# A list scheduler that may hold every engine for higher-priority work, with later weight loads and a new priority sequence, in a fused attention and MoE kernel

## The chip, the cores and the metric

The kernel runs on one core of one Trainium2 chip. Its time is the device time in microseconds (us) of one execution. Each version is executed several times, and the median is quoted with the lowest and the highest run.

A core has four computing engines, which run side by side and wait for one another by semaphores: TensorE (PE in the profile, and PEld for its weight loads), VectorE (DVE), ScalarE (ACT) and GpSimd (POOL). SyncE (SP) issues most of the DMA transfers here, and GpSimd issues the loads of the weights.

## The reference, cut to what matters

```python
# attention: batch 4, heads 8, seq 768, head_dim 64, float32
k_chunks = k.reshape(B, H, nc, 32, D)                 # 24 chunks of 32 keys
k_min, k_max = np.min(k_chunks, axis=3), np.max(k_chunks, axis=3)
ub = np.sum(np.maximum(q * k_min, q * k_max), axis=-1)     # (broadcast, cut)
ub = np.where(causal, ub, -1e9)
top_chunks = np.argsort(ub, axis=-1)[..., -6:]        # each query keeps 6 chunks
scores = scale * np.matmul(q, k.transpose(0, 1, 3, 2))
attn = softmax(np.where(selected_and_causal, scores, -1e9))
x = np.matmul(attn, v)                                # to 3072 x 512
# MoE layer: w_in 512 x 2048, w_out 2048 x 512
h = x @ w_in
g = h * np.clip(h + 3.0, 0.0, 6.0) / 6.0
return g @ w_out
```

## The kernel before

The kernel works on 16 pairs of heads and, after every four pairs, on two groups of 384 tokens of the MoE layer. It is written as about 1,100 small operations. Each has an engine, an estimated duration, the operations that it depends on and a name. A list scheduler, which runs when the kernel is built, picks the order on every engine. The names, for pair `i`:

- `k`, `q`, `v`: the loads of K, Q and V, two transfers of 192 KB each. `C` is GpSimd's cast of V.
- `K`, `Q`: transposes on TensorE (tiles KT and QT), copies to SBUF on ScalarE (KTS, QTS), and then on VectorE two reductions of K (KM, KC) and a maximum with zero of Q (QP). `B` and `R` are casts to bf16.
- `U`: the upper bounds (tile UBP). `V`: their transposes (UBQ), twelve searches for the eight largest (MAX8) and a comparison (SEL). `L`: the transposes of SEL (SLT) and a copy (SELT).
- `S`: the scores in six pieces (SPS), the exponential on ScalarE (PT) and a causal mask on GpSimd. `P`: probabilities times V (PVP), and the division (Xb).
- `X`: the transposes of the layer's input (XT), for batch 0 on TensorE and for the others by DMA. `H`: the product with w_in (HP, 8 matmuls a block), a ReLU on ScalarE and a product on VectorE (GT). `O`: the product with w_out (OP, 4 matmuls a block).
- `w0` to `w7`: the eight weight loads of 512 KB, four of w_in (WIN) and four of w_out (WOUT), issued by GpSimd.

The scheduler, with its rule for holding an engine:

```python
def run(self, slack):
    # (cut: lists of candidates for each engine)
    while any(cand.values()):
        best = None
        for eng, lst in cand.items():
            mine = None
            for op in lst:
                r = self.ready(op)
                if r is None:
                    continue
                at = max(r, self.free[eng])
                if eng == "PE" and op.mode != self.mode:
                    at += SWITCH                      # 0.095 us
                s = slack.get(eng, 0.0)
                if mine is None or (at + s < mine[0]) or (at < mine[0] + s and op.key < mine[1].key):
                    mine = (at, op)
            if mine is not None and (best is None or mine[0] < best[0]):
                best = mine
        # (cut: place the operation, take its buffers, free its successors)
...
order = plan.run(dict(PE=0.1))
```

`op.key` is the place of the operation's name in one long text, SEQUENCE. On an engine without slack, whatever can start first goes first. On an engine with slack, an operation of higher priority may make the engine wait up to that long.

The weights, the DMA transposes and the loads:

```python
WGATE = (0, 2, 1, 5, 6, 5, 6, 2)      # weight load n waits for the cast of V of this pair

def plan_weights():
    for n in range(4):
        iss = add("POOL", 0.63, f"w{n}", lambda c=c: nc.gpsimd.dma_start(WIN[...], wi[...]),
                  deps=[st[WGATE[n]]["o_v"]], chain="wi")
        res.append(add("LD", 3.1, "", None, deps=[iss], chain="w"))
    # (cut: WOUT the same, with WGATE[n + 4])

s["ldk"] = add("LD", 2.07, f"k{i}", lambda: ld(i, s["ks"], k, "KS"), take=[s["ks"]], chain="ldk")
s["ldq"] = add("LD", 2.07, f"q{i}", lambda: ld(i, s["qs"], q, "QS"), take=[s["qs"]], chain="ldq")

for t in range(TPG):                  # three DMA transposes of 128x512 bf16 for a group
    nc.sync.dma_start_transpose(xt.obj[:, t], xb[b].obj[:, blk0 + t, :])
    ops.append(add("LD", 0.7, f"X{g}.{t}", tr, deps=norms[b] + ops[:1], ...))
```

The softmax here doesn't subtract the row's maximum and nothing guards it: scores larger than these inputs give would overflow.

Of the kernel before, what the change touches and what calls it, by code (L numbers as in the profile page):

```python
# [10 lines left out]
ACT = mybir.ActivationFunctionType  # L11
# [31 lines left out]
class Plan:  # L43
# [39 lines left out]
    def run(self, slack):  # L83
        cand = {}
        after = {}
        for op in self.ops:
            op.left = len(op.deps)
            for d in op.deps:
                after.setdefault(d, []).append(op)
            if not op.left:  # L90
                cand.setdefault(op.eng, []).append(op)
        order = []
# [6 lines that stand above are left out]
                    if r is None:  # L99
                        continue  # L100
                    at = max(r, self.free[eng])
                    if eng == "PE" and op.mode != self.mode:
                        at += SWITCH
                    s = slack.get(eng, 0.0)
                    if mine is None or (at + s < mine[0]) or (at < mine[0] + s and op.key < mine[1].key):
# [3 lines that stand above are left out]
            if best is None:  # L109
                raise RuntimeError("no order")  # L110
            at, op = best
            cand[op.eng].remove(op)
            op.at, op.end = at, at + op.dur
            self.free[op.eng] = op.end
            if op.eng == "PE":
                self.mode = op.mode
            for b in op.take:
                b.slot = self.count[b.ring] % len(self.rings[b.ring])
                self.rings[b.ring][b.slot] = b
                self.count[b.ring] += 1  # L120
            for d in after.get(op, ()):
                d.left -= 1
                if not d.left:
                    cand.setdefault(d.eng, []).append(d)
            order.append(op)
        assert len(order) == len(self.ops)
        return order
# [4 lines left out]


SEQUENCE = """
H6.10 H7.14 Q10 H7.12 H7.4 P5.1 H3.6 P10.1 q15 P12.1 K9 S8.1 O6.1.8 v12 X7.2 O3.0.12 v0 H3.8 H6.14 q10 X3.2
S10.1 S11.1 K4 O3.0.4 R0 U4 L13 P10.0 U10 S9.0 P4.1 S6.4 S0.3 q14 L11 H6.0 Q15 O6.1.4 P9.1 Q5 O6.1.12 q0 v2
O3.2.0 S0.0 q2 P9.0 k10 H2.12 Q11 S5.1 V5 H7.0 S7.0 L0 X1.0 H2.14 V9 P8.0 K8 k14 H7.10 v9 H3.0 X2.1 H0.10 H3.4
v10 K0 q1 U3 S4.4 S13.1 R8 X3.1 R5 C7 H2.4 O1.2.12 C1 S0.5 S6.3 H2.10 O2.0.4 v13 K13 k1 K10 H6.12 B1 O6.0.12 R1
O4.1.0 O6.0.8 P6.0 H3.10 H1.14 X6.1 O7.0.8 O6.2.4 w5 H7.6 S12.0 V4 O6.0.0 O1.0.12 H0.14 O3.2.8 V10 B7 k9 Q14
O2.1.0 O4.2.8 H2.6 S9.3 R10 S8.5 P8.1 H0.6 S0.1 S2.1 L5 U0 H1.10 B3 S12.1 O1.0.8 K6 V2 U15 O3.1.4 C0 H1.12 K11  # L140
L4 P11.0 S0.4 S9.1 H0.0 k15 H4.0 O4.0.0 U2 Q2 P13.1 H0.2 w0 V12 H1.2 B4 U9 O0.0.12 H0.4 v3 O5.1.0 W0 S8.2 S10.2
Q8 X4.2 H0.12 H6.6 B9 O5.0.0 B15 k6 S2.2 L12 R3 P1.1 w6 X4.1 O1.1.12 O5.2.0 S7.2 k3 H6.4 W2 O4.0.12 q12 O4.1.12
q13 X3.0 S8.3 H3.12 L2 S11.4 v11 Q3 V1 S10.4 U5 O3.1.8 S14.5 O1.0.4 S6.2 L14 q7 C5 O7.1.12 k8 U8 k11 O4.1.8
O3.1.12 S14.0 O2.0.12 q8 S3.3 S6.0 Q12 Q1 S2.4 C13 P13.0 P7.0 S9.4 K1 H6.2 O1.2.4 v8 O1.1.8 V15 P15.1 O1.2.0 R12
H5.12 O5.1.12 H7.2 S5.0 v15 O2.0.8 O0.1.4 H2.2 X2.2 X1.2 X7.0 O7.1.8 k0 H2.0 R11 S11.0 S7.1 O7.2.12 B5 w7 H3.14
S1.3 S8.4 H7.8 X7.1 S14.3 S4.3 H4.8 S4.1 O4.0.4 S2.5 U6 B8 X5.2 S15.5 O2.2.0 k13 v6 S5.3 S7.5 q6 S8.0 S9.2 K15
v4 H1.8 H5.2 k2 q4 P0.1 U7 S5.4 v5 P7.1 O4.2.12 S6.5 v7 O3.1.0 O0.1.0 q5 P3.1 O1.2.8 O5.0.8 H0.8 S4.5 S7.4 S1.4
L7 V3 S3.1 O3.0.8 S1.1 V7 O0.1.12 S7.3 k7 B13 H5.10 S2.0 S3.0 P1.0 S11.5 U13 P11.1 O6.2.8 W1 V8 O4.2.4 P4.0 V13
S4.0 V11 O7.0.4 Q6 H2.8 B10 C15 k5 S13.0 X2.0 O0.0.0 U1 O2.2.8 U12 P6.1 O3.2.12 L8 L6 U14 O6.2.12 P14.0 S10.3 Q4
S5.5 S9.5 P2.0 K2 C8 w4 w3 O6.1.0 X6.2 V6 S14.1 O0.1.8 k4 S14.2 S10.0 R13 S6.1 U11 B12 P2.1 S5.2 O4.1.4 O3.0.0  # L150
S13.2 O2.1.8 P12.0 X5.1 C14 K12 O2.2.12 O2.1.12 L15 H1.6 H6.8 H3.2 L1 H5.0 K3 H4.4 V0 q11 H4.6 O2.1.4 v14 C6 L9
H4.10 O7.1.4 B6 S15.3 H4.2 C3 O6.2.0 S4.2 O7.2.0 H1.0 C10 O0.2.0 O7.1.0 X4.0 S0.2 C11 C2 B2 S11.3 O5.1.4 O4.0.8
w1 H5.14 S13.5 O6.0.4 P5.0 S10.5 S15.1 P14.1 O7.2.8 L3 K14 P0.0 H4.12 O5.1.8 R7 S12.4 S3.5 O2.0.0 S12.5 S12.3 R4
O0.0.4 K5 C9 S11.2 C12 O7.0.12 O4.2.0 S15.4 Q13 R9 R2 S12.2 O0.2.12 V14 O1.1.0 O3.2.4 S1.2 q3 X6.0 H4.14 R14 L10
B14 S3.2 R15 S3.4 B0 H1.4 X5.0 R6 q9 C4 Q0 S14.4 B11 w2 X0.0 v1 k12 H5.8 S1.5 H5.6 O1.1.4 O0.0.8 K7 P15.0 O0.2.4
O5.0.4 O5.2.4 S15.2 O5.2.8 S13.3 O1.0.0 S13.4 O0.2.8 S1.0 S15.0 O5.2.12 O2.2.4 O7.0.0 O5.0.12 Q9 H5.4 Q7 P3.0
S2.3 X0.2
"""
POS = {tok: n for n, tok in enumerate(SEQUENCE.split())}

# [6 lines left out]
def kernel(  # L167
# [21 lines left out]
    Q0 = TOPK * CH  # L189
# [11 lines left out]
    plan = Plan(rings, dict(PE=1.4, DVE=3.2, ACT=2.2, POOL=9.3, LD=0.3, ST=0.0), place)  # L201
    add = plan.add
# [88 lines left out]
                       take=[s["vs"]], chain="ldv")  # L291
        s["o_v"] = add("POOL", 0.86, f"C{i}", castv, deps=[s["ldv"]], take=[s["vb"]], use=[s["vs"]], chain="castv")

    WGATE = (0, 2, 1, 5, 6, 5, 6, 2)

    def plan_weights():
        wi = moe_w_in.rearrange("(k p) f -> p k f", p=P)
# [2 lines left out]
        for n in range(4):  # L300
            c = n * (DFF // 4)
            iss = add("POOL", 0.63, f"w{n}",
                      lambda c=c: nc.gpsimd.dma_start(WIN[:, :, c:c + DFF // 4], wi[:, :, c:c + DFF // 4]),
                      deps=[st[WGATE[n]]["o_v"]], chain="wi")
            iss.gate = n
# [13 lines left out]
        for j in range(NBLK):  # L319
            nc.tensor.transpose(T[:, j * P:(j + 1) * P], src.obj[:, j].rearrange("p e d -> p (e d)"), IDENT32[:])  # L320

    UDUR = 0.70

    def plan_K(i):
        s, tok = st[i], f"K{i}"
# [167 lines left out]
    norms = [[] for _ in range(B)]  # L493
# [39 lines left out]
    def plan_mlp(g, wdma):  # L533
        tok0 = g * GRP
        b = tok0 // S
        blk0 = (tok0 - b * S) // P
        xt, gt = Buf("xt"), Buf("gt")

        def do_xt():
            ops = []  # L540
            if b >= XDMA:
                for t in range(TPG):
                    def tr(t=t):
                        if t == 0:
                            new(xt, [P, TPG, KT_HID, P], BF16, "XT")
                        nc.sync.dma_start_transpose(xt.obj[:, t], xb[b].obj[:, blk0 + t, :])  # L546
                    ops.append(add("LD", 0.7, f"X{g}.{t}", tr, deps=norms[b] + ops[:1], take=[xt] if t == 0 else [],
                                   use=[xb[b]] if t == 0 else [xb[b], xt]))
                return ops
            for k0 in range(0, KT_HID, 2):  # L550
                ps = Buf("sm")

                def tr(k0=k0, ps=ps):
                    T = new(ps, [P, 2, GRP], BF16, "XTP")
                    for kk in range(2):
                        for t in range(TPG):
# [12 lines left out]
            return ops
# [113 lines left out]
            plan_P(i, e)  # L683
    for b in range(B):
        plan_mlp_batch(b, wdma)
    order = plan.run(dict(PE=0.1))
    done_const = False
    for n, op in enumerate(order):
        if not done_const and op.eng not in ("LD",):
# [34 lines left out]
```

## Time and profile before

| | before |
|---|---|
| time, median of 3 runs | 301.73 us (301.5 to 302.09) |
| span of the profiled execution | 300.2 us |
| TensorE busy | 96% |
| ScalarE, VectorE, GpSimd busy | 59%, 55%, 31% |

From the page of the kernel before: the busy time of each engine with its share of the span; TensorE's clock and the DMA share in 40 slices of 7.5 us each, in tenths; and the group of the HP matmuls (busy time, mean ns of one, then the idle time just before them and what ended it).

```profile
PE 287.3 (96%) x2948; PEld 178.4 (59%) x2970; DVE 163.6 (55%) x448; ACT 178.3 (59%) x219; POOL 92.5 (31%) x168
...
PEclk9959999999999999999999999999999999999999
DMA  9999999999507999762400005201011015001112
...
L578 PE MATMUL HP<-XT,WIN 128*128 128x384 bf16 x512 | 86.0, 326 | 1.4 <-DMA XT<-Xb 1.0
```

TensorE sets the time. The DMA rings are full for the first 75 us or so. One slice of the clock row shows a 5: there TensorE ran at half its clock. The view of stretches gives that stretch (its columns are the bounds, the length, busy time and instructions of PE, PEld, DVE, ACT and POOL, then the granted clock, the DMA share and GB/s).

```profile
16.40:23.20 6.80, 6.64 (x78) 3.49 (x66) 3.67 (x19) 4.15 (x5) 3.68 (x7) 0.50 1.15 183
```

The Trainium skill, "TensorE: Matmul & The Clock Gate", Part 1, says that the clock is halved after an idle window of about 3.4 us. The trace agrees as to the length: the stretch is two such windows long.

From the view of waits of the kernel before: what TensorE waited for, the us in total, how many times, and the longest one.

```profile
PE SLT L438 <- DVE SEL_130 L421: 0.9, 1, 0.9
PE QT L320 <- DMA QS<-in_q_dram: 0.8, 1, 0.8
PE KT L320 <- DMA KS<-in_k_dram: 0.3, 1, 0.3
...
PE HP L578 <- DMA XT<-Xb: 1.0, 1, 1.0
```

From the timeline of the kernel before, the prologue. Columns are the start, the busy time, the engine, the line, the operation, out<-in, the shape and the count; the bracket gives the idle time ahead of it and what ended that.

```profile
13.40 1.16 DVE L418 MAX8 T_288<-UBQ 96x8 f32<-96x24 f32 x12
...
15.05 0.44 DVE L421 TENSOR_TENSOR SEL_130<-UBQ,T_288 96x288 bf16<-96x288 f32 x1
...
15.55 0.30 PE L438 MATMUL SLT<-IDENTB,SEL_130 96*128 96x96 bf16 x3 [0.94 <-DVE SEL_130 L421]
...
17.14 0.29 DVE L442 COPY SELT<-SLT 128x288 bf16<-128x288 bf16 x1
...
18.13 1.02 ACT L479 ACTIVATE PT<-SPS 128x1024 bf16<-128x1024 f32 x1 [2.68 <-PE SPS L473]
```

This chain on VectorE decides when the first exponential may start, at 18.13 us. And from the timeline of the last third of the kernel before (SPq is SyncE's queue, which issues the DMA):

```profile
244.62 5.15 SPq L546 DMA_TRANSPOSE XT<-Xb  x4
...
249.87 0.53 SPq L613 DMA_DIRECT2D out_dram<-OT  x1
...
250.44 2.53 SPq L546 DMA_TRANSPOSE XT<-Xb  x2
...
251.15 1.46 PE L578 MATMUL HP<-XT,WIN 128*128 128x384 bf16 x8 [1.01 <-DMA XT<-Xb]
```

HP of group 6 needs three transposes. SyncE issues four before the store, because the first transpose of group 7 was put between them, and TensorE waits.

**A ledger of lost time.** Busy shares hide small holes, so the document also uses sums over TensorE's own starts. Its work is read as blocks (six transposes of K, one `U`, one `P`, eight matmuls of `H`, and so on). Each block has a nominal length: the 5th percentile of the distance from its start to the start of the next one (1298 ns for a block of `H`, 665 for `P`, 655 for the transposes of K or Q). Block by block, the start minus all nominal lengths before it is the time lost so far. The nominal sum is 263.1 us in both kernels, because they do the same matmuls. The kernel before lost the other 37.0 us, including 4 us until the first transpose.

### The profile page before, as it was taken

The numbers are of one execution on the slowest core, as the hardware profiler recorded it, in microseconds if no ns is written. First come the engines' busy times: TensorE is split into PE (matmuls) and PEld (weight loads), VectorE is DVE, ScalarE is ACT, GpSimd is POOL, SyncE is SP. The second block draws the span as 40 slices with busy tenths as digits, with TensorE's granted clock in tenths as the row PEclk, the third lists the DMA queues.
The fourth block names the chain that finished last, engine by engine and source line by source line (L and its number), as shares of the span: only waits on it lengthen the run. The fifth ranks groups of instructions, "written<-read, shape, count | busy, mean of one in ns | idle before, by whom it ended". The sixth has DMA issues, their size and how long they took to land.

```text
span 300.2 us, 7214 instructions
## 1 busy us (share of the span) xinstructions
PE 287.3 (96%) x2948; PEld 178.4 (59%) x2970; DVE 163.6 (55%) x448; ACT 178.3 (59%) x219; POOL 92.5 (31%) x168
## 2 busy tenths in 40 slices
PE   7899999999999999999999999999999998999994
PEld 7657577765666556566555664566555654655444
DVE  4768887756669876236857461468421551625300
ACT  1557798987556358755766772565567832654311
POOL 8756776662106135531220342021133100000000
PEclk9959999999999999999999999999999999999999
DMA  9999999999507999762400005201011015001112
GB/s 172 218 185 217 203 210 193 220 196 198 89 0 184 243 228 206 156 134 68 107 35 3 35 12 130 72 0 37 13 60 37 2 31 144 2 1 71 37 70 71
DMA packets 92914, 32.20 MB, mean 107 GB/s; under 512 B 85584, under 2 KB 89936, under 8 KB 92880
## 3 DMA queue, kind: packets, MB, share of 16 engines
q1 hardware_dynamic: 87088, 27.14, 42.1%
q0 software_dynamic: 4224, 4.19, 8.8%
q10 hardware_dynamic: 1568, 0.39, 0.7%
q8 instruction: 23, 0.38, 0.6%
q14 instruction: 11, 0.09, 0.1%
HBM read 27.26 MB, written 6.29 MB: 112 GB/s over the span
## 4 chain that ended last, share of the span: by engine, by line
PE 82%; DVE 4%; ACT 4%; DMA 3%; SPq 2%; issue 2%; POOL 1%; ACTq 0%; DVEq 0%; POOLq 0%
PE HP L578 28%; PE OP L604 22%; PE PVP L509 8%; PE SPS L468 7%; PE SPS L473 5%; PE UBP L388 4%; PE QT L320 3%; PE KT L320 3%; ACT PT L479 2%; PE UBQ L410 2%; SPq L546 2%; DMA XT<-Xb 2%; DMA KS<-in_k_dram 1%; PE OP L625 1%; PE SLT L438 1%
## 5 line engine op out<-in xcount | busy, mean ns | idle before, releaser
L479 ACT ACTIVATE PT<-SPS 128x1024 bf16<-128x1024 f32 (+1 forms) x96 | 82.3, 924 | 18.7 <-PE SPS L473 15.2
L588 DVE SCALAR_TENSOR_TENSOR GT<-U,HP 128x768 bf16<-128x768 bf16 x64 | 60.8, 953 | 54.4 <-ACT U L582 49.3
L578 PE MATMUL HP<-XT,WIN 128*128 128x384 bf16 x512 | 86.0, 326 | 1.4 <-DMA XT<-Xb 1.0
L604 PE MATMUL OP<-WOUT,GT 128*128 128x512 bf16 x346 | 82.6, 379 | 1.6 <-issue 0.3
L582 ACT ACTIVATE U<-HP,THREE 128x768 bf16<-128x768 f32 x64 | 57.7, 901 | 33.4 <-PE HP L578 33.2
L578 PEld LDWEIGHTS <-WIN 128*128 128x128 bf16 x512 | 49.4, 98 | 35.1 <-issue 2.2
L483 POOL TENSOR_SCALAR_AFFINE_SELECT PT<-PT 128x256 bf16<-128x256 bf16 x96 | 38.6, 408 | 73.5 <-ACT PT L479 72.9
L604 PEld LDWEIGHTS <-GT 128*128 128x128 bf16 x368 | 34.4, 98 | 39.1 <-issue 1.7
L610 ACT ACTIVATE OT<-OP 128x512 f32<-128x512 f32 x23 | 13.7, 597 | 45.4 <-PE OP L604 43.6
L468 PE MATMUL SPS<-RHS,LHS 64*128 64x512 bf16 (+3 forms) x256 | 34.5, 315 | 1.4 <-ACT PT L479 1.3
L473 PE MATMUL SPS<-SELT,EM 64*128 64x288 bf16 (+6 forms) x384 | 32.8, 253 | 0.2 <-DVE SELT L442 0.2
L509 PEld LDWEIGHTS <-PT 128*128 128x128 bf16 x672 | 23.3, 98 | 4.5 <-issue 1.5
L473 PEld LDWEIGHTS <-EM 64*128 64x128 bf16 x384 | 18.9, 96 | 8.1 <-issue 1.1
L375 POOL CAST RHS<-QTS 128x768 bf16<-128x768 f32 x16 | 15.1, 951 | 26.7 <-ACT QTS L365 26.1
L514 DVE RECIPROCAL RINV<-PVP 128x6 f32<-128x6 f32 x32 | 6.1, 192 | 30.5 <-PE PVP L509 30.3
L468 PEld LDWEIGHTS <-LHS 64*128 64x128 bf16 x256 | 11.7, 95 | 14.2 <-issue 10.7
L354 POOL CAST LHS<-KTS 128x768 bf16<-128x768 f32 x15 | 12.6, 847 | 23.0 <-ACT KTS L335 22.8
L519 DVE TENSOR_TENSOR Xb<-PVP,RINV 128x384 bf16<-128x384 f32 x32 | 17.7, 555 | 0.9
L365 ACT COPY QTS<-QT 128x768 f32<-128x768 f32 x16 | 12.4, 802 | 6.6 <-PE QT L320 5.1
L339 DVE TENSOR_REDUCE KM<-KTS 128x24 f32<-128x768 f32 x15 | 13.9, 943 | 4.4 <-ACT KTS L335 4.3
L335 ACT COPY KTS<-KT 128x768 f32<-128x768 f32 x15 | 11.9, 807 | 5.2 <-PE KT L320 5.2
L320 PE MATMUL KT<-IDENT_114,KS 128*128 128x128 f32 x96 | 13.5, 284 | 0.5 <-DMA KS<-in_k_dram 0.3
(113 smaller groups left out, 233.6 us busy)
## 6 DMA issues: line engine op xcount, KB each, us to landing
VS<-in_v_dram SPq DMA_DIRECT2D x32, 192.0 KB, 4.6
KS<-in_k_dram SPq DMA_DIRECT2D x31, 192.0 KB, 4.5
QS<-in_q_dram SPq DMA_DIRECT2D x31, 192.0 KB, 4.5
out_dram<-OT SPq DMA_DIRECT2D x23, 256.0 KB, 2.0
WIN<-in_moe_w_in_dram POOLq DMA_DIRECT2D x4, 512.0 KB, 7.2
WOUT<-in_moe_w_out_dram POOLq DMA_DIRECT2D x4, 512.0 KB, 10.9
XT<-Xb SPq DMA_TRANSPOSE x18, 2.5
out_dram<-OT SPq DMA_DIRECT2D x2, 128.0 KB, 1.7
```

The lines of the kernel that those rows point to most:

```text
L320: nc.tensor.transpose(T[:, j * P:(j + 1) * P], src.obj[:, j].rearrange("p e d -> p (e d)"), IDENT32[:])
L375: nc.gpsimd.tensor_copy(new(s["rhs"], [P, S], BF16, "RHS")[:], qts.obj[:])
L468: nc.tensor.matmul(T[:, e, c:c + hi - lo], lhsT=s["lhs"].obj[e * D:(e + 1) * D, j * P:(j + 1) * P], rhs=s["rhs"].obj[e * D:(e + 1) * D, lo ...
L473: nc.tensor.matmul(T[:, e, c:c + hi - lo], lhsT=EM[e * D:(e + 1) * D, h, j * P:(j + 1) * P], rhs=s["selt"].obj[e * D:(e + 1) * D, x:x + hi ...
L479: nc.scalar.activation(T[:, :, 0:w], sp.obj[:, :, 0:w], ACT.Exp, scale=scale)
L483: nc.gpsimd.affine_select(out=dv, in_=dv, pattern=[[0, 2], [1, P]], compare_op=A.is_ge, fill=0.0, base=0, channel_multiplier=-1)
L509: nc.tensor.matmul(T[:, qb, :], lhsT=t[:, e, c:c + P], rhs=fx(s["vb"])[:, e, j, :], start=(j == 0), stop=(j == qb))
L519: nc.vector.tensor_tensor(out=xb[b].obj[:, :, h * D:(h + 1) * D], in0=pv.obj[:, :, 0:D], in1=s[("ri", e)][:].to_broadcast([P, NBLK, D]), o ...
L578: nc.tensor.matmul(T[:, f, 0:GRP].rearrange("p (t s) -> p t s", s=P), lhsT=WIN[:, kt, (f0 + f) * P:(f0 + f + 1) * P], rhs=xt.obj[:, :, kt, ...
L582: nc.scalar.activation(new(u, [P, 2, GRP], BF16, "U")[:], hp.obj[:, :, 0:GRP], ACT.Relu, bias=THREE[:], scale=1.0)
L588: nc.vector.scalar_tensor_tensor(out=gt.obj[:, f0:f0 + 2, :], in0=u.obj[:], scalar=6.0, in1=hp.obj[:, :, 0:GRP], op0=A.min, op1=A.mult)
L604: nc.tensor.matmul(T[:, :], lhsT=gt.obj[:, f, t * P:(t + 1) * P], rhs=WOUT[:, f, :], start=(f == 0), stop=(f == FT - 1))
```

## The change

The intent is that any engine may wait shortly for a part of higher priority, not only TensorE; that the loads of K, Q and V have the DMA rings to themselves early, so the first weights come after the fourth cast of V; that loads which could start together follow their priority (a hold of 0.01 us); and that a new sequence, searched for under these rules, is used. Three durations of the plan were corrected as well: `U`, the DMA transposes (0.7 to 1.3 us), and the cost of a change of TensorE's mode.

```diff
 LAT = {"PE": 0.22, "DVE": 0.09, "ACT": 0.09, "POOL": 0.09, "LD": 2.0, "ST": 2.0}
 SWITCH = 0.095
+SLACK = dict(PE=0.1, ACT=0.15, DVE=0.15, POOL=0.15, LD=0.01)
...
-                    if eng == "PE" and op.mode != self.mode:
+                    if eng == "PE" and self.mode not in (op.mode, 2):
                         at += SWITCH
...
 SEQUENCE = """
-H6.10 H7.14 Q10 H7.12 H7.4 P5.1 H3.6 P10.1 q15 P12.1 K9 S8.1 O6.1.8 v12 X7.2 O3.0.12 v0 H3.8 H6.14 q10 X3.2
+S3.2 q2 q1 O4.1.4 k13 O7.0.4 H3.2 P4.1 H7.12 P10.1 P6.0 U14 P5.0 O3.0.0 H3.8 R5 S0.5 O7.0.12 w0 H7.10 O7.1.8
 (some 20 lines cut: every name has a new place)
-    WGATE = (0, 2, 1, 5, 6, 5, 6, 2)
+    WGATE = (3, 1, 3, 5, 3, 1, 3, 0)
-    UDUR = 0.70
+    UDUR = 0.60
-                    ops.append(add("LD", 0.7, f"X{g}.{t}", tr, ...
+                    ops.append(add("LD", 1.3, f"X{g}.{t}", tr, ...
-    order = plan.run(dict(PE=0.1))
+    order = plan.run(SLACK)
```

What the engines then do early, by the order of instructions:

```
            before                                      after
TensorE     ... V0 K2 Q2 L0 U1 S0.3 S0.0 S0.5 ...       ... V0 K2 L0 Q2 U1 S0.5 S0.1 S0.2 ...
VectorE     ... U0 K1 K1 V0 Q1 K1 V0 K2 K2 L0 ...       ... U0 K1 V0 V0 K1 K1 Q1 L0 K2 U1 ...
ScalarE     B0 Q0 K1 ...                                Q0 B0 K1 ...
GpSimd      ... R2 C0 w0 S0.3 ...                       ... C2 B5 S1.4 (6 masks) C3 w0 R4 w1 ...
SyncE       ... k2 q2 v0 k3 q3 v1 k4 q4 v2 ...          ... k2 q2 v0 k3 v1 k4 q3 k5 v2 ...
```

More of the change, by code (lines that the diff above doesn't have):

```diff
@@ L134 @@
 SEQUENCE = """
-H6.10 H7.14 Q10 H7.12 H7.4 P5.1 H3.6 P10.1 q15 P12.1 K9 S8.1 O6.1.8 v12 X7.2 O3.0.12 v0 H3.8 H6.14 q10 X3.2
-S10.1 S11.1 K4 O3.0.4 R0 U4 L13 P10.0 U10 S9.0 P4.1 S6.4 S0.3 q14 L11 H6.0 Q15 O6.1.4 P9.1 Q5 O6.1.12 q0 v2
-O3.2.0 S0.0 q2 P9.0 k10 H2.12 Q11 S5.1 V5 H7.0 S7.0 L0 X1.0 H2.14 V9 P8.0 K8 k14 H7.10 v9 H3.0 X2.1 H0.10 H3.4
-v10 K0 q1 U3 S4.4 S13.1 R8 X3.1 R5 C7 H2.4 O1.2.12 C1 S0.5 S6.3 H2.10 O2.0.4 v13 K13 k1 K10 H6.12 B1 O6.0.12 R1
-O4.1.0 O6.0.8 P6.0 H3.10 H1.14 X6.1 O7.0.8 O6.2.4 w5 H7.6 S12.0 V4 O6.0.0 O1.0.12 H0.14 O3.2.8 V10 B7 k9 Q14
@@ L140 @@
-O2.1.0 O4.2.8 H2.6 S9.3 R10 S8.5 P8.1 H0.6 S0.1 S2.1 L5 U0 H1.10 B3 S12.1 O1.0.8 K6 V2 U15 O3.1.4 C0 H1.12 K11
-L4 P11.0 S0.4 S9.1 H0.0 k15 H4.0 O4.0.0 U2 Q2 P13.1 H0.2 w0 V12 H1.2 B4 U9 O0.0.12 H0.4 v3 O5.1.0 W0 S8.2 S10.2
-Q8 X4.2 H0.12 H6.6 B9 O5.0.0 B15 k6 S2.2 L12 R3 P1.1 w6 X4.1 O1.1.12 O5.2.0 S7.2 k3 H6.4 W2 O4.0.12 q12 O4.1.12
-q13 X3.0 S8.3 H3.12 L2 S11.4 v11 Q3 V1 S10.4 U5 O3.1.8 S14.5 O1.0.4 S6.2 L14 q7 C5 O7.1.12 k8 U8 k11 O4.1.8
-O3.1.12 S14.0 O2.0.12 q8 S3.3 S6.0 Q12 Q1 S2.4 C13 P13.0 P7.0 S9.4 K1 H6.2 O1.2.4 v8 O1.1.8 V15 P15.1 O1.2.0 R12
@@ L145 @@
-H5.12 O5.1.12 H7.2 S5.0 v15 O2.0.8 O0.1.4 H2.2 X2.2 X1.2 X7.0 O7.1.8 k0 H2.0 R11 S11.0 S7.1 O7.2.12 B5 w7 H3.14
-S1.3 S8.4 H7.8 X7.1 S14.3 S4.3 H4.8 S4.1 O4.0.4 S2.5 U6 B8 X5.2 S15.5 O2.2.0 k13 v6 S5.3 S7.5 q6 S8.0 S9.2 K15
-v4 H1.8 H5.2 k2 q4 P0.1 U7 S5.4 v5 P7.1 O4.2.12 S6.5 v7 O3.1.0 O0.1.0 q5 P3.1 O1.2.8 O5.0.8 H0.8 S4.5 S7.4 S1.4
-L7 V3 S3.1 O3.0.8 S1.1 V7 O0.1.12 S7.3 k7 B13 H5.10 S2.0 S3.0 P1.0 S11.5 U13 P11.1 O6.2.8 W1 V8 O4.2.4 P4.0 V13
-S4.0 V11 O7.0.4 Q6 H2.8 B10 C15 k5 S13.0 X2.0 O0.0.0 U1 O2.2.8 U12 P6.1 O3.2.12 L8 L6 U14 O6.2.12 P14.0 S10.3 Q4
@@ L150 @@
-S5.5 S9.5 P2.0 K2 C8 w4 w3 O6.1.0 X6.2 V6 S14.1 O0.1.8 k4 S14.2 S10.0 R13 S6.1 U11 B12 P2.1 S5.2 O4.1.4 O3.0.0
-S13.2 O2.1.8 P12.0 X5.1 C14 K12 O2.2.12 O2.1.12 L15 H1.6 H6.8 H3.2 L1 H5.0 K3 H4.4 V0 q11 H4.6 O2.1.4 v14 C6 L9
-H4.10 O7.1.4 B6 S15.3 H4.2 C3 O6.2.0 S4.2 O7.2.0 H1.0 C10 O0.2.0 O7.1.0 X4.0 S0.2 C11 C2 B2 S11.3 O5.1.4 O4.0.8
-w1 H5.14 S13.5 O6.0.4 P5.0 S10.5 S15.1 P14.1 O7.2.8 L3 K14 P0.0 H4.12 O5.1.8 R7 S12.4 S3.5 O2.0.0 S12.5 S12.3 R4
-O0.0.4 K5 C9 S11.2 C12 O7.0.12 O4.2.0 S15.4 Q13 R9 R2 S12.2 O0.2.12 V14 O1.1.0 O3.2.4 S1.2 q3 X6.0 H4.14 R14 L10
@@ L155 @@
-B14 S3.2 R15 S3.4 B0 H1.4 X5.0 R6 q9 C4 Q0 S14.4 B11 w2 X0.0 v1 k12 H5.8 S1.5 H5.6 O1.1.4 O0.0.8 K7 P15.0 O0.2.4
-O5.0.4 O5.2.4 S15.2 O5.2.8 S13.3 O1.0.0 S13.4 O0.2.8 S1.0 S15.0 O5.2.12 O2.2.4 O7.0.0 O5.0.12 Q9 H5.4 Q7 P3.0
-S2.3 X0.2
+S3.2 q2 q1 O4.1.4 k13 O7.0.4 H3.2 P4.1 H7.12 P10.1 P6.0 U14 P5.0 O3.0.0 H3.8 R5 S0.5 O7.0.12 w0 H7.10 O7.1.8
+X7.2 H7.4 W2 k7 q6 O6.0.12 H0.10 w5 P4.0 H3.4 V9 U6 U1 O4.0.12 U5 S0.1 O7.2.0 P15.0 H7.14 k11 S14.2 S5.1 S6.1
+U10 v0 P0.1 Q7 H2.8 P1.0 k1 Q3 k3 B4 Q10 P7.0 B3 S7.0 O7.2.12 H1.12 O5.2.12 O3.2.8 K10 S1.3 R3 U7 H0.6 P11.1 C2
@@ new lines @@
+P8.1 H1.2 P13.0 S7.5 H1.8 U2 Q8 L8 S7.2 q11 R4 C15 H3.0 S4.0 L1 S4.1 H7.8 S10.0 V3 S7.1 k0 v6 S12.1 S9.5 X4.2
+S12.5 S14.1 S1.1 S13.4 v3 S8.4 C7 P3.0 S4.2 S4.3 S10.2 O6.0.8 L12 O6.2.8 q0 H7.2 k10 S7.4 S6.4 X3.0 U8 X4.0 B12
+V0 S11.2 Q6 O5.1.0 R15 H2.0 S14.5 S1.2 K1 O6.0.0 X3.2 v1 V5 O0.2.12 L6 S5.5 O3.2.12 P10.0 O0.2.4 U4 U13 K15 H6.4
+S11.3 v7 U0 Q1 K5 k4 S2.3 R2 S14.4 B10 H2.12 q12 S9.0 q3 O7.2.8 R9 O7.0.8 U11 H5.14 X7.0 S12.2 w1 P2.0 H6.6
+O2.0.8 O0.1.8 K12 L5 X1.2 B7 L11 B15 q14 R7 C4 H2.6 O1.2.8 P5.1 Q5 H1.4 H5.8 S3.3 S10.3 V2 H3.6 U3 O3.2.4 P9.0
@@ new lines @@
+V15 S8.1 Q2 P11.0 w3 S6.0 X0.0 U9 P3.1 H1.10 S2.1 S3.5 S7.3 H0.2 V4 S9.1 P12.0 P9.1 H2.4 P14.0 L9 v11 S0.2 R10
+P2.1 H3.14 V1 q9 H6.12 C0 C1 v5 H1.6 L4 S10.4 S3.1 v10 H6.2 W0 H0.8 S10.5 S9.3 H0.12 O7.0.0 k8 H1.0 H1.14 R13 C6
+S3.4 S1.5 q5 U12 q8 Q0 P14.1 V7 S9.2 S6.3 P12.1 O7.1.0 X2.1 O6.0.4 X0.2 H3.12 S15.3 S5.4 S2.0 O2.1.12 H6.8
+O4.0.0 O1.2.12 O0.0.8 S3.0 S14.0 w7 H0.4 v4 q10 L0 S8.0 v2 S1.0 R8 k6 H7.6 O2.2.4 S15.4 H5.0 S8.5 H7.0 S2.5 S5.0
+S2.2 S2.4 R12 C3 H2.2 S10.1 H0.14 O1.0.4 Q4 H4.14 O5.2.8 L7 K7 O7.1.12 K2 X3.1 Q11 S0.3 S5.3 v8 S0.4 L2 O1.1.4
@@ new lines @@
+O6.1.8 V13 Q14 O1.0.12 P15.1 Q15 O5.2.0 B9 S15.0 v12 S9.4 O1.0.8 O3.1.0 S14.3 S11.1 O4.2.0 O4.0.4 O1.0.0 B5 S5.2
+q4 O6.1.12 H0.0 P8.0 L10 O4.2.4 H3.10 V10 X4.1 P0.0 C9 O1.2.0 O1.2.4 P13.1 X6.2 K3 w6 O3.0.8 H5.6 V6 O4.1.0 w2
+P7.1 X6.1 K0 k5 O0.0.0 V11 H5.10 X7.1 S8.2 K4 S11.4 S0.0 O6.2.12 B6 R14 v15 k14 P6.1 O5.0.12 S13.5 R1 O4.0.8
+X2.2 P1.1 H2.10 B11 S6.2 H2.14 B1 O3.1.8 U15 O2.0.4 X1.0 S6.5 K9 X5.0 k2 O4.2.8 O4.2.12 C11 L14 O0.1.0 v13 V8
+L15 S15.1 O2.1.4 H6.0 K6 K14 B14 S13.3 K8 O2.1.0 O4.1.12 S4.5 O1.1.8 Q9 H6.10 O3.2.0 X2.0 S8.3 L3 B0 O5.0.4
@@ L158 @@
+O5.2.4 O2.0.0 B2 C10 S12.3 S13.0 O3.1.4 S13.1 O7.1.4 k15 O2.2.12 B13 C5 R11 H4.0 S12.4 S12.0 q7 S1.4 O2.2.0 v9
+v14 O0.1.12 O2.2.8 w4 S11.0 O6.1.0 C13 S13.2 K11 S15.2 q15 q13 k9 O5.0.0 L13 X5.2 O5.1.8 V14 H5.2 O3.0.12
+O1.1.12 C8 X6.0 R0 R6 k12 O5.0.8 H4.10 S11.5 O0.2.0 W1 S15.5 O0.2.8 O3.0.4 K13 V12 Q13 O2.0.12 O0.0.12 C12
+O1.1.0 X5.1 O3.1.12 B8 O0.1.4 C14 O6.2.0 H5.12 H4.2 Q12 O6.2.4 H5.4 S4.4 H4.6 H4.8 O5.1.12 O6.1.4 O5.1.4 H6.14
+H4.4 O2.1.8 H4.12 O4.1.8 O0.0.4
 """
@@ L546, in tr @@
                         nc.sync.dma_start_transpose(xt.obj[:, t], xb[b].obj[:, blk0 + t, :])
-                    ops.append(add("LD", 0.7, f"X{g}.{t}", tr, deps=norms[b] + ops[:1], take=[xt] if t == 0 else [],
+                    ops.append(add("LD", 1.3, f"X{g}.{t}", tr, deps=norms[b] + ops[:1], take=[xt] if t == 0 else [],
                                    use=[xb[b]] if t == 0 else [xb[b], xt]))
```

## The prediction

> **What bounds the kernel now.** TensorE. The page gives PE 96% of 300.2 us, ACT 59%, DVE 55%, POOL 31%; the clock is full after 40 us. By the stretches view PE is busy 41.6 of 43 us (17-60), 180.3 of 183 (60-243), 52.0 of 58 (243-301). But the Trainium skill ("Trainium Kernel Development and Optimization", Performance Expectations) calls matmul busy time a bad metric because matmuls are pipelined, and this trace agrees: the starts of consecutive matmuls, each held against the usual distance after the same shape (162 ns for 128x384, 216 for 128x512, 109 for the f32 transposes), leave about 27 us in holes over 140 ns and 23 us in small ones. 14 and 10 us of these lie in the first 60 us. The small ones are largely changes between full-array and 64-row matmuls: after a 128x512 the next starts at 311 instead of 216 ns when it is a 64-row one.
>
> The matmul work is the same in both kernels. Only holes, prologue and tail can give.
>
> **What the change moves (from the order of instructions), costed.**
> 1. Prologue. ACT now copies QTS before LHS. Before, QTS waited behind the 0.80 us LHS copy and UBP started at 10.18. KT on PE (to about 9.7) then limits, so UBP gains 0.45 us. DVE now runs the first max8 and SEL comparison after one KM reduction rather than after KM, KC (0.94 each) and QP; SELT comes before both reductions of pair 2 (0.93 each). From 10.75: bias 0.5, KM 0.9, max8 1.1, compare 0.4, KC, difference and QP 1.5, SELT 0.3: the first masked scores at about 15.6 instead of 17.48, so the first exp at about 16.3 instead of 18.13. Gain about 1.8 us, of which I count 1.3 as kept.
> 2. Weights. The first WIN load moves from 17.06 us to about 40 us, behind the fourth cast. Now it shares the rings with loads: v of pair 1 landed 20.75 and 24.18, instead of 0.9 apart. "DMA: Bandwidth & Descriptors" (Issuing engines are not separate DMA queues) says so too. But PE hardly waits for DMA (1.0+0.8+0.3 us), so only about 0.3 us gained; pair 3's q comes later, without a wait that I can see.
> 3. Transposes by DMA. The plan now uses 1.3 us (trace: 1.20-1.28 each). After the last PVP, HP of group 6 waited: hole of 1.18 us at 249.7, after 8 blocks of OP. Now 13 blocks (11 us) cover five transposes, one store and the landing (about 9.6 us). Gain 1.2 us; the same at 187.7, 0.3 us.
> 4. Mode changes on PE: 115 to 111 by the order; at 95 ns, 0.4 us.
> 5. The other holes (0.2-0.9 us each, such as 0.88 at 229 behind an OT copy, 0.5 each at 97 and 98 in the burst of K) are re-dealt by the new order. I expect 1 us net gain, very uncertain.
>
> Added work: none.
>
> **Sum** -4.2 us: 297.5 us. Range 293.5 to 301.5. Faster by over 2% 0.23, within 2% 0.75, slower 0.02.
>
> **What the profile would show.** First UBP near 9.7 and first exp near 16.3; no WIN issue before 35 us; first HP at 57.5-61 (was 60.5); no wait of HP for XT over 0.3 us after the last PVP; PE busy total changed by less than 4 us; ACT, DVE totals the same.
>
> **What would make it wrong.** Up to the first HP, ACT (35.7 of 43 us busy) may eat the earlier prologue. WIN and WOUT issued closer together (about 40 to 62 us) could land late and hold HP or OP. Fewer attention pieces left for later could make denser HP runs wait for GT or U. Or the search found much more in the middle (over 60 us: 26 us of holes) than I can see from the order: then under 294.

## The result, and the profile after

| | before | after |
|---|---|---|
| time, median of 4 runs each, same rounds | 301.62 us (301.32 to 302.09) | 296.3 us (296.1 to 296.73) |
| span of the profiled execution | 300.2 us | 294.5 us |
| granted clock in that execution | 0.988 | 0.997 |

The ratio is 0.9824, with a 95% interval from 0.9807 to 0.9841. A ratio here is the mean time of one kernel's fast runs over that of the other's of the same rounds, so it is not quite the ratio of the medians. The change is 1.8% faster, within 2%. It was run again beside the experiments below and gave 0.9809.

The same lines of the page, after (all line numbers are one higher):

```profile
PE 282.8 (96%) x2947; PEld 177.1 (60%) x2970; DVE 165.4 (56%) x448; ACT 177.9 (60%) x219; POOL 91.9 (31%) x168
...
PEclk9999999999999999999999999999999999999998
DMA  9999999899972377997110043110000053011012
...
L579 PE MATMUL HP<-XT,WIN 128*128 128x384 bf16 x512 | 86.5, 326 | 0.2 <-DMA XT<-Xb 0.2
```

TensorE is 96% busy in both kernels, so this share says nothing of where 5.7 us of span went. The Trainium skill, "Trainium Kernel Development and Optimization", Performance Expectations, calls matmul busy time a bad metric because matmuls are pipelined. The half-clock stretch is gone, and so is most of HP's wait for XT. After, TensorE's waits are these:

```profile
PE SLT L439 <- DVE SEL_130 L422: 1.1, 1, 1.1
PE UBP L389 <- DVE QP L370: 1.0, 3, 0.5
PE PVP L510 <- DVE Xb L520: 0.8, 1, 0.8
PE KT L321 <- DMA KS<-in_k_dram: 0.4, 1, 0.4
...
PE HP L579 <- DMA XT<-Xb: 0.2, 1, 0.2
```

The wait for Q is gone. A hole of 0.8 us and three for QP are new. The new order does not only remove holes.

The prologue after:

```profile
12.29 1.16 DVE L419 MAX8 T_275<-UBQ 96x8 f32<-96x24 f32 x12
...
13.49 0.45 DVE L422 TENSOR_TENSOR SEL_130<-UBQ,T_275 96x288 bf16<-96x288 f32 x1
...
14.00 0.30 PE L439 MATMUL SLT<-IDENTB,SEL_130 96*128 96x96 bf16 x3 [1.07 <-DVE SEL_130 L422]
...
15.30 0.30 DVE L443 COPY SELT<-SLT 128x288 bf16<-128x288 bf16 x1
...
16.57 2.35 ACT L480 ACTIVATE PT<-SPS 128x256 bf16<-128x256 f32 x3 [0.76 <-PE SPS L474]
```

The first exponential starts 1.56 us earlier. And the start of group 6 after:

```profile
235.10 11.38 PE L605 MATMUL OP<-WOUT,GT 128*128 128x512 bf16 x51
...
235.96 3.81 SPq L547 DMA_TRANSPOSE XT<-Xb  x3
...
240.45 2.53 SPq L547 DMA_TRANSPOSE XT<-Xb  x2
...
246.32 1.95 PE L579 MATMUL HP<-XT,WIN 128*128 128x384 bf16 x11
```

More blocks of OP now lie between the last PVP and the first HP of group 6 (13 instead of 8), and they cover the transposes. The order of the transposes is no better than before: two of group 7 are now issued among the first three, so that five have to go out before group 6 has its own.

The ledger of the two profiled executions, in us lost since the start:

| mark | before | after | gained in this stretch |
|---|---|---|---|
| first UBP | 6.20 | 5.96 | 0.24 |
| first PVP | 13.23 | 10.16 | 2.83 |
| first HP | 19.34 | 16.39 | -0.12 |
| last PVP | 29.69 | 25.38 | 1.36 |
| first HP of group 6 | 31.25 | 25.55 | 1.39 |
| end | 37.04 | 31.36 | -0.02 |

The gains add up to 5.68 us, which is the difference of the spans. The first HP itself starts at 57.17 us instead of 60.52. So there are three places to explain: 2.95 us before the first HP, 1.36 us in the long middle and 1.39 us after the last PVP.

### The profile page after: what moved, and what is told of

Its sections match the earlier page's. It is cut to its first block, busy times and chain, and to the rows that moved or that the text cites. A ratio compares the mean times of both kernels' runs of the same rounds, so it can differ in the third digit from the quotient of the medians.

```text
span 294.5 us, 7206 instructions
## 1 busy us (share of the span) xinstructions
PE 282.8 (96%) x2947; PEld 177.1 (60%) x2970; DVE 165.4 (56%) x448; ACT 177.9 (60%) x219; POOL 91.9 (31%) x168
## 4 chain that ended last, share of the span: by engine, by line
PE 86%; DVE 8%; DMA 3%; issue 1%; ACT 1%; SPq 0%; ACTq 0%; DVEq 0%
PE HP L579 28%; PE OP L605 27%; PE PVP L510 6%; PE SPS L469 6%; PE SPS L474 4%; PE UBP L389 4%; PE KT L321 3%; PE QT L321 2%; DMA XT<-Xb 2%; PE UBQ L411 2%; DMA KS<-in_k_dram 1%; PE OP L626 1%; DVE QP L370 1%; DVE UBT L397 1%; DVE Xb L520 1%
## 5 line engine op out<-in xcount | busy, mean ns | idle before, releaser
L469 PE MATMUL SPS<-RHS,LHS 64*128 64x128 bf16 (+3 forms) x256 | 33.7, 307 | 0.6 <-ACT PT L480 0.4
L474 PE MATMUL SPS<-SELT,EM 64*128 64x288 bf16 (+6 forms) x384 | 31.8, 247 | 0.0
L474 PEld LDWEIGHTS <-EM 64*128 64x128 bf16 x384 | 18.1, 94 | 7.3
L469 PEld LDWEIGHTS <-LHS 64*128 64x128 bf16 x256 | 11.1, 94 | 12.8 <-issue 9.9
L397 DVE TENSOR_TENSOR UBT<-UBP,BIAS 96x384 f32<-96x384 f32 x16 | 8.8, 553 | 10.0 <-PE UBP L389 9.7
```

Of the source, the lines that this page charges most:

```text
L469: nc.tensor.matmul(T[:, e, c:c + hi - lo], lhsT=s["lhs"].obj[e * D:(e + 1) * D, j * P:(j + 1) * P], rhs=s["rhs"].obj[e * D:(e + 1) * D, lo ...
L474: nc.tensor.matmul(T[:, e, c:c + hi - lo], lhsT=EM[e * D:(e + 1) * D, h, j * P:(j + 1) * P], rhs=s["selt"].obj[e * D:(e + 1) * D, x:x + hi ...
```

## The experiments

**How single parts were undone.** The scheduler's order was written out as a fixed list of operations, in place of the search. The list of the kernel before, written out so, builds to the same program as the kernel before on every engine. Then one engine's order, or one operation's place, can be changed alone. The diffs below show the changed engine's list of names; all other engines keep theirs. Every kernel gave a correct result. The theory at the outset was the prediction's: an earlier first exponential, a little from the weights, the transposes. The rivals were that the clock was the main cause in the prologue, and that the DMA rings were.

The first four kernels ran on one chip, where the kernel before took 301.46 us (301.2 to 301.86, 11 runs).

### b_fill: is it the clock?

Dummy matmuls fill the holes of the prologue of the kernel before, so that TensorE does not look idle.

```diff
+add("PE", 0.8, "F", fill(7), ...)     # 7 matmuls IDENT x IDENT, f32, after K2
+add("PE", 0.9, "F", fill(8), ...)     # 8 more, after Q2
```

> The kernel before with its exact order on every engine, plus 15 dummy matmuls (f32 identity, 0.11 us each, as in its own warm-up) in the two holes of TensorE at 12.7-13.8 and 14.4-15.5 us. Clock theory: the half clock of 16.4-23.2 us in the trace of before comes from these holes; with them filled the clock stays at full speed, the lost PE time up to the first PVP falls by 1.5 to 3 us, and the whole by about as much (299-300 us). Rival, earlier-start theory: the clock matters little because ACT and DVE pace this stretch; the whole changes by less than 0.5 us although the clock record shows no half-speed stretch.

Measured: 302.94 us (302.0 to 303.97), ratio 1.0051 [1.0035, 1.0067]. The profiled execution had the full clock. From its timeline (TensorE alone; WRM is the filler):

```profile
13.22 1.73 PE L692 MATMUL WRM<-IDENT 128*128 128x128 f32 x14
...
15.44 1.95 PE L692 MATMUL WRM<-IDENT 128*128 128x128 f32 x16
17.22 0.29 PE L438 MATMUL SLT<-IDENTB,SEL 96*128 96x96 bf16 x3
```

The experiment was badly sized. Each f32 matmul is two instructions, so the filler was twice as long as planned; SLT started at 17.22 us instead of 15.55, and about that was lost. Its own time therefore says little. The kernel before answers the question better. Of its 11 runs on this chip, four had a mean clock of 1.0 and took 301.33 us on average; four had 0.993 or 0.994 and took 301.58. The difference of about 0.25 us is of the size of their scatter. (A mean of 0.993 to 0.994 is about one window of 3.4 us at half the clock. On the other two chips the runs of the kernel before with 0.992 to 0.994 took 302.10 and 301.91 us on average, the others 302.17 and 301.91.) The profiled execution, with two such windows, took 301.9 us, against 301.5 to 302.09 for the runs beside it. So a half-clock stretch costs little, and the clock is not the main cause of a gain of over 5 us.

### b_dve: VectorE's early order alone

```diff
 VectorE
-... U0 K1 K1 V0 Q1 K1 V0 K2 K2 L0 Q2 U1 ...
+... U0 K1 V0 V0 K1 Q1 K1 L0 K2 K2 Q2 U1 ...
```

> The kernel before, with only VectorE's order changed for the first pairs: max8 and the SEL comparison of pair 0 before the second reduction of pair 1, and the SELT copy before the reductions of pair 2. All other engines' orders are the same. Earlier-start theory: first exp at about 16.5 us instead of 18.1, and the whole 1.0 to 1.6 us shorter. Clock theory: the hole before SLT shrinks by over 1 us; if the clock then stays at full speed the whole gains 2.5 to 3 us, if it still falls to half at 16.4 us the gain is under 1 us.

Measured: 301.41 us (300.74 to 301.76), ratio 0.9992 [0.998, 1.0004]: nothing. Yet the first exponential did start earlier, at 17.09 us. Its timeline and its waits show where the gain went:

```profile
24.31 0.30 PE L438 MATMUL SLT<-IDENTB,SEL 96*128 96x96 bf16 x3
26.04 0.85 PE L320 MATMUL KT<-IDENT,KS 128*128 128x128 f32 x6 [1.42 <-DMA KS<-in_k_dram]
```

```profile
PE KT L320 <- DMA KS<-in_k_dram: 1.7, 2, 1.4
```

TensorE waits 1.42 us for K of pair 4, which lands at 25.90 us. In the kernel before the same load landed at 26.22 us and TensorE came to it only at 26.88:

```profile
26.88 0.87 PE L320 MATMUL KT<-IDENT_114,KS 128*128 128x128 f32 x6
```

So the load is the limit. The profile of the kernel before did not show that, as its TensorE was late, with half its clock from 16.4 to 23.2 us. Why the load is late can be read from the records of the issues:

```
                    before              b_dve          after
v of pair 1 landed  20.75, 24.18        20.91, 21.65   19.32, 20.14
first WIN issued    17.06               17.04          37.40
first WIN landed    23.63               24.71          44.94
k of pair 4 landed  25.32, 26.22        25.04, 25.90   20.91, 21.94
q of pair 3 landed  19.26, 20.00        18.13, 18.99   22.84, 23.63
```

Loads land some 0.9 us apart until the first WIN load joins them; then there is a gap of 3.4 us. The Trainium skill, "DMA: Bandwidth & Descriptors" (section "Issuing engines are not separate DMA queues"), says that all issuers share the same 16 DMA engines and interleave. That agrees with these times.

### b_prolog: the whole new beginning

All engines take the order of the kernel after up to the first PVP, and then what is left in the order of the kernel before.

```diff
 TensorE
-... K2 Q2 L0 U1 S0.3 S0.0 S0.5 V1 S0.1 S0.4 U2 L1 Q3 V2 K3 ... P0.0
+... K2 L0 Q2 U1 S0.5 S0.1 S0.2 V1 S0.3 S0.4 K3 L1 U2 S0.0 V2 ... P0.0   (then as before)
 (the other engines likewise; the first WIN load is issued at 23.49 us)
```

> The order of after on all engines up to the first PVP of pair 0, from there the order of before. If the gain of the prologue (3.07 us by the first PVP in the traces) is kept by the rest whatever its order, the whole is 2.5 to 3.1 us shorter than before, about 298.9. If ACT eats it, under 1.5 us. The first WIN load goes out at about 22 us here, not at 17, so this also moves that part of the weights.

Measured: 304.37 us (303.92 to 305.21), ratio 1.0099 [1.0086, 1.0112], slower. At the seam the two orders do not fit: on VectorE the comparison of pair 2 came to stand behind the QP of pair 3, and TensorE waited 1.75 us for it at 27.05 us. This is an artefact of the splice. It says only that the head of one order with the tail of another does not carry the gain over.

### b_xswap: the transposes in front of group 6

```diff
 SyncE
-... X5.2 X6.0 X7.0 X6.1 X6.2 X7.1 X7.2
+... X5.2 X6.0 X6.1 X6.2 X7.0 X7.1 X7.2
```

> The kernel before with one DMA transpose of group 7 issued after the three of group 6 instead of between them; every other order the same. If the hole of 1.18 us before the HP matmuls of group 6 is the wait for its third transpose, which stood one place too far back in the queue of SP, it falls to about 0.1 us and the whole is 1.0 to 1.2 us shorter. If the matmuls waited for something else (a GT or HP buffer), nothing changes.

Measured: 300.76 us; five runs lie between 300.26 and 300.98, and one took 303.77. With it the ratio is 0.999 [0.996, 1.0019], so by the times this is not shown to be faster, although five of its six runs lie below the fastest of the 11 runs of the kernel before (301.2). In the trace the effect is plain:

```profile
244.21 5.14 SPq L546 DMA_TRANSPOSE XT<-Xb  x4
...
249.56 1.46 PE L578 MATMUL HP<-XT,WIN 128*128 128x384 bf16 x8
```

HP of group 6 starts 1.59 us earlier than in the kernel before, no longer with a wait for XT that the timeline shows. By the ledger the loss between the last PVP and this HP fell from 1.56 to 0.38 us. The prologue of this kernel is that of the kernel before, and in this execution only half of the half-clock stretch occurred (0.77 of the clock on average from 16.4 to 23.2 us). There TensorE was again early enough to wait for the load:

```profile
26.37 0.84 PE L320 MATMUL KT<-IDENT,KS 128*128 128x128 f32 x6 [1.16 <-DMA KS<-in_k_dram]
```

The next four kernels ran on a second chip, on which runs scattered more: the kernel before took 302.12 us (301.36 to 303.61, 11 runs).

### b_w0, b_dve_w0: the first weight load later, in the old order

```diff
 GpSimd (b_w0; b_dve_w0 has the VectorE order of b_dve as well)
-... R2 C0 w0 S0.3 ... C2 S1.5 S1.0 w1 S2.1 ...
+... R2 C0 S0.3 ... C2 S1.5 S1.0 w0 w1 S2.1 ...
```

> The kernel before with one instruction moved: the issue of the first WIN load goes on GpSimd from behind the first cast of v to just before the second WIN load (about 35 us instead of 17). Theory of the pair (DMA rings and the DVE order hide each other): k of pair 4 lands about 3 us earlier, but TensorE does not reach it earlier, so the whole changes by less than 0.5 us. Rival (weights alone were the early limit): 1 us or more shorter.

> Both: VectorE's order as in b_dve, which alone changed nothing, and the first WIN load moved as in b_w0. Theory of the pair: the wait of 1.6 us of TensorE for k of pair 4 that b_dve shows at 24.3 us goes away, and the whole is 1.0 to 1.6 us shorter than before (300.0 to 300.5). Rival (the early stretch is paced by ACT and nothing there is worth time): less than 0.5 us.

Measured: b_w0 302.08 us (300.42 to 304.09), ratio 1.0000 [0.9965, 1.0035]. Its profiled execution began slowly (the first UBP at 12.12 us), so its early stretch can't be compared; K of pair 4 did land some 2.8 us earlier (22.49 and 23.39 us). b_dve_w0 took 302.22 us (299.86 to 304.24), ratio 1.0004 [0.9964, 1.0044]. Neither is worth anything within about 0.4%. The trace of b_dve_w0 shows that the wait for K of pair 4 did go: K landed at 22.98 and 23.84 us, and the lost time at the first PVP is 11.23 us against 12.35 in b_dve. But 25 us later it was given back. Three WIN loads were now issued close together (33.35, 34.22 and 35.33 us), V of pair 4 landed at 42.33 and 47.66 us, and its cast stood on GpSimd in front of the masks that the PVP of pair 3 needed:

```profile
47.79 0.84 POOL L288 CAST VB<-VS 128x768 bf16<-128x768 f32 x1 [0.94 <-DMA VS<-in_v_dram]
...
48.57 1.50 POOL L483 TENSOR_SCALAR_AFFINE_SELECT PT<-PT 128x256 bf16<-128x256 bf16 x4
49.03 0.92 PE L509 MATMUL PVP<-VB,PT 128*128 128x65 bf16 x16 [0.50 <-POOL PT L483]
```

At the first HP, b_dve_w0 had lost 18.57 us and b_dve 18.46. The wait moved, it did not vanish. (The kernel after bunches these loads too, at 37.40, 39.05 and 40.15 us, and its V of pair 4 lands at 42.05 and 47.42. But there the cast runs only at 51.78 us, after the masks of pair 3, and TensorE does not wait for it.)

### b_dve_w0_x: the three moves together

```diff
 GpSimd and VectorE as in b_dve_w0, SyncE as in b_xswap
```

> The kernel before with the three hand moves together: VectorE's order, the first WIN load, the DMA transpose of group 7 behind those of group 6. If the gains add: about 1.3 us from the first two and 0.8 to 1.1 us from the third, 299.0 to 299.6. If the tail's gain is eaten: like b_dve_w0.

Measured: 299.95 us (299.76 to 302.15), ratio 0.994 [0.9912, 0.9968]. Since b_dve_w0 alone gave nothing, the gain probably goes with the swapped transposes; the two intervals just overlap, but the ledger has a loss of 0.37 us in front of HP of group 6, as in b_xswap. Three moves by hand give 0.6%, a third of what the new order gives.

### a_w0 and a_w0_again: the first weight load early, in the new order

This is the kernel after with the first WIN load put back behind the first cast. It ran on the second chip, and again on a third beside a second run of the kernel after (there the kernel before took 301.86 us, 301.37 to 302.79, 11 runs).

```diff
 GpSimd
-... S0.5 C0 S0.1 S0.2 ... S2.4 C3 w0 R4 w1 ...
+... S0.5 C0 w0 S0.1 S0.2 ... S2.4 C3 R4 w1 ...
```

> The kernel after with the first WIN load issued early, behind the first cast of v, as before did; nothing else moved. Theory of the pair: the loads of pairs 3 to 5 land about 3.4 us later, TensorE, which is earlier in this kernel, waits for q of pair 3 or k of pair 5, and 1.5 to 3 us are lost (297.8 to 299.3). Rival, as predicted blind: the move of the weights is worth 0.3 us, so 296.6 at most.

> The changed kernel with the first WIN load issued early, a second time, beside the changed kernel. The trace of its first run shows TensorE waiting 2.0 us for q of pair 3. If that wait is typical, the median is 1 to 2.3 us above that of the run beside it; if the first trace caught a bad landing, under 0.5 us.

> The changed kernel itself, on the same chip as the three runs beside it: 0.980 to 0.985 of before, and the same 0.9824 as in its first runs if the noise of the chip that ran the last group does not come back.

Measured on the second chip: a_w0 297.53 us (296.7 to 300.54), ratio 0.9857 [0.9817, 0.9897]. On the third chip: after_again 296.18 us (295.89 to 296.46), ratio 0.9809 [0.9793, 0.9825], and a_w0_again 297.76 us (296.96 to 301.38), ratio 0.9878 [0.984, 0.9916]. The two intervals do not overlap. The medians differ by 1.6 us, and the spans of the two profiled executions by 1.3 us (296.1 and 294.8). From the timeline of a_w0_again:

```profile
26.89 0.84 PE L320 MATMUL QT<-IDENT,QS 128*128 128x128 f32 x6 [1.48 <-DMA QS<-in_q_dram]
```

and from that of the kernel after:

```profile
25.16 0.85 PE L321 MATMUL QT<-IDENT_114,QS 128*128 128x128 f32 x6
```

Q of pair 3 landed at 25.91 and 26.75 us with the early weights, and at 22.84 and 23.63 without. The wait is not made up later. In the ledger, a_w0_again is 1.60 us behind after_again at the first PVP of pair 1 and 1.61 us behind at the first HP. In the new order the place of the first weight load is worth about 1.5 us.

### seq_only: the new sequence under the old rules

```diff
-SEQUENCE = (old)
+SEQUENCE = (new)          # slack, gates, durations and mode rule as before
```

> The kernel before with the new sequence alone: old hold rule (TensorE only), old weights gates, old durations. The order that comes out differs from that of after at most places, so if the sequence is worth something only with the settings it was searched under, this is no faster than before, and probably slower (300 to 306). If the sequence itself carries the gain: 297 or less.

Measured: 314.87 us (313.73 to 316.78), ratio 1.0435 [1.0406, 1.0464], slower. From its waits:

```profile
PE QT L320 <- DMA QS<-in_q_dram: 4.3, 3, 2.9
PE SLT L438 <- DVE SEL L421: 3.4, 3, 1.5
```

The sequence was searched for under the new rules, and is bad under the old ones. Most of the rest of this decomposition could not be run. With the new sequence and a hold for TensorE only, with a hold for TensorE and the loads only, with the new gates but the old hold, with the old sequence under all new settings, and with the old sequence under the new settings but the old gates, the scheduler found no legal order at all (the buffers ran into one another), so there was no kernel. What the hold rule, the gates and the sequence are worth each by itself stays open. (The kernel after without the hold of the loads does build, and so does the kernel before with the new gates alone; neither was run.)

### a_tuned: can the kernel after be bettered by hand?

The largest hole of the kernel after in the middle lies at 94.2 us (0.92 us lost, behind the division Xb). In this kernel a block of HP of group 1 was moved from 84.8 us into it, blocks of OP moved up into the place that it left, and at 61 us a copy of Q was put ahead of a ReLU.

```diff
 TensorE
-O0.0.0 H1.14 U8 S6.2 O0.0.4 O0.0.8 S6.5 S7.0 S7.5 V8 S7.2 O0.0.12 S7.1 S7.4 S7.3 P6.0 L8 P6.1
+O0.0.0 O0.0.4 O0.0.8 U8 S6.2 O0.0.12 S6.5 S7.0 S7.5 V8 S7.2 P6.0 H1.14 P6.1 L8 S7.1 S7.4 S7.3
 ScalarE
-S5.2 H0.0 Q7 H0.2
+S5.2 Q7 H0.0 H0.2
 (ScalarE's and VectorE's lists follow TensorE's)
```

> The changed kernel with two of its remaining holes moved by hand: the Q copy of pair 7 before the first relu on ACT and VectorE (TensorE waits 0.56 us for QP at 61.7), and one HP block of group 1 moved from 84.8 us to between the two PVP of pair 6, which stand 0.92 us apart at 94.2 because both need the same small PSUM buffers. If holes on TensorE are the time, 0.5 to 1.4 us shorter than the changed kernel beside it. If the slack elsewhere is what they were bought with, no change.

Measured: 296.38 us (295.88 to 296.55), ratio 0.9814 [0.9797, 0.9831], and after_again on the same chip has 0.9809: no change. The hole at 94.2 us went, and one of 0.90 us appeared between the last two pieces of scores of pair 7, where TensorE now waits for ScalarE. The hole at 61 us stayed. No version was found that beats the kernel after.

## Why the prediction was right or wrong

The total was right: 297.5 us was predicted with a range from 293.5 to 301.5, 296.3 was measured, and the most likely class, "within 2%", came true, if narrowly. (The prediction's terms as written add up to 4.5 us, not to the 4.2 that it took off.) The split of the sum was wrong. That it came so close is partly luck: the order's part of the prologue was taken 0.6 us too large and the weights 1.2 us too small (points 1 and 2), which partly cancel.

A forecast was also at hand in the kernels themselves: the scheduler's own plan ends at 299.4 us before and at 293.5 us after (the scheduler alone), 5.9 us apart. The two plans use different durations for U and the transposes, so this agreement too may be partly chance.

**1. The prologue, "1.3 as kept": right in mechanism, smaller by itself.** The first UBP started at 9.93 us (said: near 9.7) and the first exponential at 16.57 (said: near 16.3). But b_dve shows that an earlier exponential alone is worth nothing, because TensorE then stands before a load. How much is kept can be read at the first HP. The ledger has 19.34 us lost in the profiled execution of the kernel before, and 18.81 in b_xswap, which is the same program up to there with less of the half clock. It has 18.12 in a_w0_again (the new order with early weights) and 16.51 in after_again. So about 0.5 us of the 2.95 that the two profiles show is the half clock of one execution, about 0.7 us belongs to the new order, and 1.6 us to the weights. (These are differences of single traced executions. b_xswap still had one window of half clock, so the first part may be larger and the second smaller.)

**2. The weights, "only about 0.3 us": this is the step that failed, by a term mis-sized about five times.** It measured about 1.5 us (a_w0_again against after_again: 1.6 by the medians, 1.3 by the spans). The prediction sized it by the waits that it saw ("PE hardly waits for DMA (1.0+0.8+0.3 us)"). But a wait that is seen now is not what a resource is worth after the change. The loads came just in time for a TensorE that was late for other reasons; as soon as it was earlier, the ring became the next limit. The prediction had even seen that V of pair 1 landed 3.4 us apart, and had the right page for it. Its guess about Q of pair 3, "without a wait that I can see", held in the kernel after; the kernel with early weights shows the wait of 1.48 us which that avoided.

The runs show the two parts to be complements, at least as moved here:

| ratio to before | first WIN load early (17 to 19 us) | first WIN load late (33 us or later) |
|---|---|---|
| old order | 1 | 1.0000 (b_w0) |
| old order, VectorE's beginning new | 0.9992 (b_dve) | 1.0004 (b_dve_w0) |
| new order | 0.9878 (a_w0_again) | 0.9809 (after_again) |

Each ratio is to the kernel before on the same chip. Two cautions: the intervals of b_w0 and b_dve_w0 are 0.35 to 0.4% wide to each side, so a gain of up to 1 us there is not excluded. And in the old order the late load was bunched with two others, with a cast of V waiting in front of masks, and that cost time at 48 us. So the right column of the old order is the value of this move, not of the best one.

**3. The DMA transposes, "Gain 1.2 us": right.** The ledger gives 1.39 us between the last PVP and HP of group 6, and HP's wait for XT fell from 1.0 to 0.2 us. b_xswap, which changes only the order of the transposes, gets 1.18 us of that in its trace (1.56 to 0.38). Its times did not confirm it by themselves. It shows that the hole was the wait for the transposes; the kernel after closes it in another way, by covering them with more blocks of OP, as the prediction said, and that was not tested alone. The further 0.3 us at 187.7 us is in the ledger as well: 0.27 us were lost in front of the first HP of group 4 before, and about 0.01 after.

**4 and 5. "Mode changes ... 0.4 us" and "1 us net gain, very uncertain": the sum fits, the parts are not shown.** From the first HP to the last PVP the ledger gained 1.36 us. The holes of over 0.25 us a block add up to 2.77 us before and 2.53 after, so hardly anything came from large holes as a whole: those that the prediction named (at 97, 98 and 229 us) are gone, but others opened (0.56 us at 61 and 0.92 at 94). The other 1.1 us is spread over small excesses. Four or five fewer mode changes at 95 ns could be 0.4 us of it; no run tells that apart. a_tuned shows how such holes behave: one filled by hand opened another.

**The signs.** No WIN load was issued before 35 us (37.40), HP waited 0.2 us at most for XT after the last PVP, and ACT and DVE totals stayed (178.3 and 177.9 us; 163.6 and 165.4). The first HP came at 57.17 us, just earlier than the said 57.5 to 61. One sign was badly chosen: PE busy was to change by less than 4 us and fell by 4.5. With the same matmuls, the busy time takes in small holes and half-clock matmuls, so it follows the span. Of the dangers that were named, the weights did come close together in the kernel after, but neither HP nor OP waited for them; in b_dve_w0 it was a cast of V, and so a PVP, that paid.

## What to carry to other kernels

Don't size a shared resource by the waits that the present profile shows: ask what will stand before it once the other limit is lifted, and test both changes in a two by two, because each alone may be worth nothing. When all engines keep one order that was searched for as a whole, a part of it taken over alone, or a hole filled by hand, tends to move the loss to another place. To find where time went on an engine that is "96% busy" in both versions, add up the distances between the starts of its own blocks against a nominal length, and compare at marks that both versions pass.

## What the Trainium skill lacked or had wrong

- "Advanced Engine Details and Errata", X-Bar Transpose (TRN2), says that transposing DMAs are as fast as regular ones, and gives 350 to 400 GB/s. Here SBUF to SBUF transposes of 128x512 bf16 (131 KB) took SyncE 1.20 to 1.28 us each to issue, landed about 2.5 us after the issue, and landed 1.28 to 1.34 us apart when issued in a row: about 100 GB/s, as SyncE issues them (whether the issue or the transfer sets this pace is not shown). The plain 192 KB loads landed about 0.9 us apart, about 220 GB/s.
- "DMA: Bandwidth & Descriptors" says that issuers share the engines, but has no figure for what a large load through GpSimd does to loads queued by SyncE. One 512 KB WIN load opened a gap of 3.4 us between two landings of 192 KB that were otherwise 0.9 us apart, and with it early in the new order Q of pair 3 landed 3.1 us later.
- "TensorEngine Tiling (Array Packing)", Key Properties, says that a change of mode drains TensorE, without a size. Here the matmul after a 128x512 one started 311 ns later when the mode changed, and 216 ns later when it did not: 95 ns.
- "TensorE: Matmul & The Clock Gate", Part 1, ties the half clock to an idle window, without saying how little work counts as idle. Here TensorE was busy for 1.70 of the 3.4 us before the halving (16.4 us), and b_xswap had the same (1.71 of 3.41 us before 16.14). The stretch was in some executions of the same program and not in others, and runs with one window of it were at most some 0.25 us longer. With less of it, TensorE waited 1.2 to 1.4 us for a load that the half-clocked execution did not have to wait for. The page does not say that a halved clock can hide such a wait.
